# Routed experts: weights in 18 slots instead of two halves, the low halves on VectorE and ScalarE alone, and the code of a single tile ahead of that of a pair

## The chip, the cores and the metric

The kernel runs on one core of one Trainium2 chip. The metric is the time of one execution on the device in microseconds (us); of several executions the median counts. The engines are TensorE (PE for products, PEld for loading their stationary side), VectorE (DVE), ScalarE (ACT), GpSimd (POOL) and SyncE (SP), which issues most transfers. Each runs an instruction stream of its own, in order, and waits on counters (semaphores) that the others raise.

## What is computed

Three stages follow each other: attention with a memory term (4 x 8 heads, 576 rows of 64), a layer of eight experts, and a gated layer.

```python
logits = x @ w_gate                      # x: 2304 tokens x 512
e_idx = np.argmax(logits, axis=1)
for e in range(8):
    mask = e_idx == e
    h = np.maximum(x[mask] @ w1[e], 0.0)         # 512 -> 1024
    ye = h @ w2[e]                               # 1024 -> 512
    out[mask] = gate_w[mask, None] * eom[mask, e, None] * ye
...
gate = 1.0 / (1.0 + np.exp(-(x @ w_gate)))       # 512 -> 1536
return (gate * (x @ w_val) @ w_out)
```

How many tokens an expert has is known only on the device. With these inputs the eight experts have 2, 465, 120, 834, 36, 680, 12 and 155 tokens, that is 1, 4, 1, 7, 1, 6, 1 and 2 tiles of 128.

## The kernel before

All products run on values split in two fp32r halves, a high one (ScalarE copies it, line 1159) and a low one (the rest, a subtraction, line 1166); three products (high x high, high x low, low x high) stand for one. The weights of an expert are eight parts of 128 x 1024: four of w1, four of w2. Each is loaded to one of seven raw buffers, and split to the two halves (`split_hi`, `split_lo`). Two large tiles W[0] and W[1] hold the halves, of even and of odd experts. While expert e runs, the eight parts of expert e + 1 are split (`splits`, `split_part`); of eight low halves POOL takes three (parts 2, 4 and 7) and DVE five. After the last expert's turn come parts of the gated layer's weights (`early_parts`: six parts are converted from 64 bits during expert 7, `convert` on DVE, line 1204 to 1210, low halves on POOL, line 1218).

An expert's tiles run in pairs, and an odd last one alone. `pair` has 152 products, `single` 64 (four layer-1 groups of six, then layer 2, with the turns of h and of the next x between them); with the weight loads that is some 304 and 128 instructions of PE. Both begin with the gather of the next x tiles by POOL (`load_x`, lines 1260 to 1262), turn these tiles near their end (`x_turn`, lines 1270 to 1274) and end with `store_y`: ACT scales the first tile (line 1281), DVE the second (line 1283), and SP stores. In `single` the splits stand at fixed places: SG = (0, 3, 2, 3, 1, 3, 1) steps of `splits` after the loads, after the first relu, in the middle of the second layer-1 group, and so on.

The branches are nested per expert (line 1445): if it has more than one tile, `pair` and then `rest(e, 1)`, which asks at line 1412 whether anything is left, then whether two are; `else` branches with `single` stand behind the whole nest, in reverse order. So in the instruction streams an expert's code is: first pair, second, third and fourth pair, a loop that serves experts of more than eight tiles, and then the single-tile codes. An expert of one tile jumps over all of that, and one with an even number of tiles jumps from its last pair to the nest's end, from there behind the single codes, and on.

The framework counts each engine's finished instructions through all branches. On a path that leaves a block out, each engine waits until its own count is reached (its earlier work is finished) and adds the block's number; SP does the same for the counters of its transfers. This is called a pad here. Code behind a branch waits for the highest count among the paths; if the path taken left that work out, it waits for the pad of the engine that would have done it.

The first single tile's code (expert 0) follows a part of the attention stage in which parts 6 and 7 of expert 0 are split by POOL as one instruction each, part 1 as four (line 672).

Of the kernel before, what the change touches and what calls it, by code (L numbers as in the profile page):

```python
# [18 lines left out]
P = 128  # L19
# [7 lines left out]
NE = 8  # L27
# [99 lines left out]
class Attention:  # L127
# [385 lines left out]
    def run(self, ex, change):  # L513
# [153 lines left out]
        for n in range(8):  # L667
# [4 lines left out]
                lambda e, n=n: ex.split_lo(n, *((self.nc.vector, 1) if e == "DV" else (self.nc.gpsimd, 4 if n < 2 else 1))), needs=[("wh", n)] + late)  # L672
# [401 lines left out]
class Experts:  # L1074
# [67 lines left out]
    def hi_lo(self, part):  # L1142

        kind, a, i = part
        if kind == "e":
            w = self.W[a % 2]
            o = i * 1024 if i < 4 else 8192 + (i - 4) * 1024
            return w[:, o : o + 1024], w[:, o + 4096 : o + 5120]
        n = 3 * i + a
        w, n = (self.Wx, n) if n < 4 else (self.W[0], n - 4) if n < 20 else (self.W[1], n - 20)  # L1150
        o = n * 1024
        return w[:, o : o + 512], w[:, o + 512 : o + 1024]
# [62 lines left out]
    def split(self, n, lo, eng=None):  # L1215
# [26 lines left out]
    def experts(self, ids, cum, start, xn, gather):  # L1242
        tc, nc = self.tc, self.nc
        with ExitStack() as ctx:
# [46 lines left out]


            def layer1(w, n, ms):
                for m in ms:
                    a, o = ((xh, 0), (xh, 4096), (xl, 0))[m // 4]
                    c = o + m % 4 * 1024 + n * 512
                    nc.tensor.matmul(  # L1297
                        pH[n], lhsT=a[:, m % 4, 0:P], rhs=w[:, c : c + 512], start=(m == 0), stop=(m == 11)
# [9 lines left out]
            def layer2(w, n, ms):  # L1308
                for m in ms:
                    a, o = ((hh, 8192), (hh, 12288), (hl, 8192))[m // 4]  # L1310
                    k = m % 4
                    c = o + (n * 4 + k) * 512
                    nc.tensor.matmul(
                        pY[0], lhsT=a[n][:, k * P : (k + 1) * P], rhs=w[:, c : c + 512],
# [3 lines left out]
            def single(e, i, k, splits=iter(())):  # L1318
                w = self.W[e % 2]
# [29 lines left out]
                split(99 * (e == NE - 1))  # L1349


            def inner(w, f):
                p = (*pH, *pT)[f % 4][:, 0 : 2 * P]
                for m in range(12):
                    a, o = ((xh, 0), (xh, 4096), (xl, 0))[m // 4]
                    c = o + m % 4 * 1024 + f * P
                    nc.tensor.matmul(p, lhsT=w[:, c : c + P], rhs=a[:, m % 4, :], start=(m == 0), stop=(m == 11))
# [5 lines left out]
            def outer(w, f):  # L1363
                for t in range(2):
                    q = f % 2 * 256 + t * P
                    for m, (a, o) in enumerate(((hh, 8192), (hh, 12288), (hl, 8192))):
                        nc.tensor.matmul(
                            pY[t], lhsT=a[f % 4 // 2][:, q : q + P], rhs=w[:, o + f * 512 : o + (f + 1) * 512],
# [3 lines left out]
            def pair(e, i, k, splits=iter(()), lead=False):  # L1372
                w = self.W[e % 2]
# [25 lines left out]
            def splits(e):  # L1399
# [4 lines left out]
                for n in range(8):  # L1404
                    self.split_part()
                    yield
                    if n % 2 == 0:
                        yield

            def rest(e, j):  # L1410

                with tc.If(cum[e + 1] > cum[e] + 2 * j):
                    if j > AHEAD:
# [4 lines left out]
                        return  # L1418
# [20 lines left out]
            with tc.manual_schedule():  # L1439
                x_turn(0)  # L1440
                for e in range(NE):
                    if e == NE - 1:
                        first_load()
                    state = dict(self.at), list(self.free), self.loads, self.done
# [304 lines left out]
```

## Time and profile before

| | |
|---|---|
| three runs | 1103.66, 1106.94, 1111.60 us; median 1106.94 us |
| the profiled execution | 1110.49 us, of which the span of the trace is 1108.6 us |
| expert stage in it | about 310 us to 629 us of the span |
| PE busy | 1028.2 us (93%) |
| DVE, ACT, POOL busy | 525.0, 456.2 and 289.1 us |

The trace gives each instruction's start and length, and what ended the idle time of its engine before it. "issue" there is idle time in which the engine waited for nothing that the profile shows. "L1297" is line 1297 of the kernel. The queue named q8 carries PE's instructions in blocks of 16 KB, which is 256 instructions; q14 carries blocks of 8 KB.

### The profile page before, as it was taken

How to read it: one execution, taken by the hardware profiler on the slowest of the kernel's cores; microseconds unless marked ns; L12 is line 12 of the kernel's file. 1: busy time of each engine (PE TensorE's matmuls, PEld its weight loads, DVE VectorE, ACT ScalarE, POOL GpSimd, SP SyncE). 2: the span in 40 equal slices, each digit the busy share in tenths (PEclk: the TensorE clock that was granted, in tenths of full speed). 3: DMA queues.
4: the chain of work that ended last, by engine and by line, in shares of the span. 5: the costliest groups of instructions: out<-in, count | busy, mean ns of one | idle time of the engine just before them, and what ended most of it. 6: DMA issues, size and time to landing. Idle time of an engine off the chain costs nothing. (4 is left out here: it accounts for less than half of the span.)

```text
span 1108.6 us, 17069 instructions
## 1 busy us (share of the span) xinstructions
PE 1028.2 (93%) x6181; PEld 878.6 (79%) x6181; DVE 525.0 (47%) x1263; ACT 456.2 (41%) x1049; POOL 289.1 (26%) x396
## 2 busy tenths in 40 slices
PE   6899899999869699989979789999999999999997
PEld 4567566666559589968968689999899999999996
DVE  5877677676564163246216799931212122121111
ACT  5687686876444253236224455521212221221211
POOL 8677446231374152035115200000100100100101
PEclk9899999999879899999999889999999999999999
DMA  6637445321277164138225455500110100100000
GB/s 123 130 99 172 104 85 131 73 66 36 75 261 257 44 236 136 39 91 295 73 66 149 162 175 196 159 1 1 38 48 1 58 1 1 57 1 1 30 1 28
DMA packets 111899, 102.49 MB, mean 92 GB/s; under 512 B 69520, under 2 KB 86928, under 8 KB 111760
## 3 DMA queue, kind: packets, MB, share of 16 engines
q1 hardware_dynamic: 107888, 88.18, 27.7%
q0 software_dynamic: 3872, 12.62, 3.6%
q8 instruction: 68, 1.11, 0.4%
q14 instruction: 71, 0.58, 0.2%
HBM read 84.49 MB, written 16.28 MB: 91 GB/s over the span
## 5 line engine op out<-in xcount | busy, mean ns | idle before, releaser
L1546 DVE TENSOR_TENSOR G<-G,pT 128x384 f32<-128x384 f32 (+1 forms) x74 | 40.1, 542 | 249.0 <-PE pT L1532 247.5
L1578 POOL DMA_INDIRECT out_dram<-o,rows x18 | 17.5, 971 | 461.7 <-ACT o L1574 212.5
L1553 ACT ACTIVATE Gh<-G 128x384 fp32r<-128x384 f32 (+1 forms) x74 | 38.2, 516 | 162.1 <-DVE G L1546 162.0
L1542 ACT ACTIVATE G<-pH 128x384 f32<-128x384 f32 x72 | 35.4, 491 | 132.4 <-PE pH L1532 132.3
L415 ACT ACTIVATE Sm<-Sm,mx 128x512 f32<-128x512 f32 (+3 forms) x144 | 83.2, 579 | 14.1 <-DVE mx L407 13.6
L407 DVE CUSTOM_DVE_ANT_0 Sm<-Sp,mask 128x512 f32<-128x512 f32 (+3 forms) x144 | 65.2, 481 | 19.6 <-PE T L460 8.1
L1166 POOL TENSOR_TENSOR W<-raw,W 128x1024 fp32r<-128x1024 f32 (+1 forms) x25 | 56.7, 2274 | 66.8 <-ACT W L1159 66.8
L460 PE MATMUL T<-ident,Sm 128*128 128x128 f32 (+1 forms) x400 | 61.2, 287 | 8.9 <-ACT xt L304 3.2
L1563 PE MATMUL pX<-W,Gh 128*128 128x512 f32 x220 | 68.9, 394 | 0.0
L1159 ACT ACTIVATE W<-raw 128x1024 fp32r<-128x1024 f32 x60 | 61.7, 1054 | 13.8 <-DMA y_dram<-y 6.5
L460 PEld LDWEIGHTS T<-ident,Sm 128*128 128x128 f32 (+1 forms) x400 | 44.3, 142 | 21.0 <-ACT xt L304 4.0
L1166 DVE TENSOR_TENSOR W<-raw,W 128x1024 fp32r<-128x1024 f32 x38 | 56.9, 1508 | 6.8 <-ACT W L1159 6.8
L494 PE MATMUL O<-pt,vn 128*64 128x192 f32 (+4 forms) x512 | 59.7, 353 | 0.0
L304 ACT ACTIVATE pt<-T 128x512 f32<-128x512 f32 (+4 forms) x128 | 49.3, 434 | 24.5 <-PE T L460 24.0
L1551 DVE TENSOR_TENSOR Gl<-G,Gh 128x384 fp32r<-128x384 f32 (+1 forms) x74 | 40.4, 546 | 33.9 <-ACT Gh L1553 33.9
L1532 PE MATMUL pT<-xh,W 128*128 128x384 f32 x264 | 52.8, 343 | 2.0 <-DVE G L1546 2.0
L1532 PE MATMUL pT<-yh,W 128*128 128x384 f32 x264 | 51.3, 336 | 0.0
L378 PE MATMUL Sp<-kz,qT 64*128 64x512 f32 (+3 forms) x384 | 49.0, 361 | 1.9 <-DVE kz L351 0.8
L1532 PEld LDWEIGHTS pT<-xh,W 128*128 128x128 f32 x264 | 47.4, 192 | 3.0 <-DVE G L1546 2.2
L1297 PE MATMUL pH<-W,xh 128*128 128x512 f32 x80 | 26.4, 472 | 24.8 <-issue 24.3
L1532 PE MATMUL pH<-yh,W 128*128 128x384 f32 x240 | 47.0, 337 | 1.4 <-DVE xl L1521 1.4
L494 PEld LDWEIGHTS O<-pt,vn 128*64 128x64 f32 (+1 forms) x512 | 30.6, 137 | 21.6 <-issue 13.7
(336 smaller groups left out, 2457.8 us busy)
## 6 DMA issues: line engine op xcount, KB each, us to landing
raw<-in_moe_w_dram SPq DMA_DIRECT2D x60, 512.0 KB, 5.1
raw<-in_moe_w_gate_dram SPq DMA_DIRECT2D x12, 512.0 KB, 5.9
raw<-in_moe_w_val_dram SPq DMA_DIRECT2D x12, 512.0 KB, 3.7
raw<-in_moe_w_out_dram SPq DMA_DIRECT2D x12, 512.0 KB, 4.6
y_dram<-y SPq DMA_DIRECT2D x9, 513.0 KB, 3.5
qn<-in_q_dram SPq DMA_DIRECT2D x32, 128.0 KB, 2.6
kn<-in_k_dram SPq DMA_DIRECT2D x32, 128.0 KB, 2.7
zf<-in_z_prev_dram SPq DMA_DIRECT2D x32, 128.0 KB, 5.3
```

Of the source, the lines that this page charges most:

```text
L304: self.nc.scalar.activation(out, in_, AF.Copy)
L378: nc.tensor.matmul(Sp[:, j, 0:n], lhsT=q[r, a, c * 128 : (c + 1) * 128], rhs=kz[r, k, 0:n], start=(p_ == 0), stop=(p_ == 2), skip_group_ch ...
L407: self.nc.vector.tensor_tensor_reduce(out=self.Sm[pi, n][:, k0:k1], in0=self.Sp[pi, c][:, j if n < 8 else si, 0 : k1 - k0], in1=mask, scal ...
L415: self.nc.scalar.activation(self.Sm[pi, n], self.Sm[pi, n], AF.Exp, scale=-1.0, bias=self.mx[pi, n][:, si : si + 1], accum_out=self.sums[p ...
L460: nc.tensor.transpose(T[:kr, o * 128 : (o + 1) * 128], self.Sm[pi, n][:, i * 128 : i * 128 + kr], self.ident)
L494: nc.tensor.matmul(O[j * 64 : (j + 1) * 64, q0 - q0b : q1 - q0b], lhsT=self.G[gi, "v"][:kr, i, 2 * l + j, :], rhs=PT[:kr, j, i, q0:q1], st ...
L1159: self.nc.scalar.activation(hi, t, AF.Copy)
L1166: eng.tensor_tensor(lo[:, o : o + w], t[:, o : o + w], hi.bitcast(F32)[:, o : o + w], ALU.subtract)
L1532: nc.tensor.matmul(t, lhsT=w[:, k * P : (k + 1) * P], rhs=x[:, k, :], start=(m == k == 0), stop=(m == 2 and k == 3),)
L1546: nc.vector.tensor_tensor(t, t, p, ALU.mult)
L1551: nc.vector.tensor_tensor(l, t, hi.bitcast(F32), ALU.subtract)
L1563: nc.tensor.matmul(po[g][jj], lhsT=a[:, ts], rhs=w, start=(f == 0 and m == 0), stop=(f == NF - 1 and m == 2), skip_group_check=True,)
```

## The change

Four things change. First, the two weight tiles and the small tile Wx become 18 slots of one part each, used in turn; the splits run up to ten parts ahead instead of eight: expert 1 splits ten parts, experts 2 to 5 eight each, expert 6 the last six, so that the first two parts of the next but one expert are always done. Second, all low halves in this stage go to DVE, the early parts of the gated layer too; POOL keeps only parts 1, 6 and 7 of expert 0, and takes each of them in four instructions. Third, `rest(e, 0)` replaces the nest: for each j first "exactly one tile left: `single`", then "two or more left: `pair`, and `rest(e, j + 1)`", two branches in a row without an `else`. Fourth, at the start of `single` and of `pair` each engine gets an instruction that announces where a coming branch will jump (`jump`): from `single` over the pair's code, from `pair` over the next pair's code if no two tiles will be left.

```diff
-                lambda e, n=n: ex.split_lo(n, *((self.nc.vector, 1) if e == "DV" else (self.nc.gpsimd, 4 if n < 2 else 1))), needs=[("wh", n)] + late)
+                lambda e, n=n: ex.split_lo(n, *((self.nc.vector, 1) if e == "DV" else (self.nc.gpsimd, 4))), needs=[("wh", n)] + late)
...
-            w = self.W[a % 2]
-            o = i * 1024 if i < 4 else 8192 + (i - 4) * 1024
-            return w[:, o : o + 1024], w[:, o + 4096 : o + 5120]
+            return self.slot(8 * a + i)
+
+        n = 20 + 3 * i + a
+        o = n % 2 * 512
+        return [t[:, o : o + 512] for t in self.slot(n // 2)]
+
+    def slot(self, n):
+
+        n %= 18
+        w, n = (self.W[n // 8], n % 8) if n < 16 else (self.Wx, n - 16)
+        return w[:, n * 2048 : n * 2048 + 1024], w[:, n * 2048 + 1024 : (n + 1) * 2048]
...
-        self.split_lo(n, self.nc.gpsimd if n % 8 in (2, 4, 7) else self.nc.vector)
+        self.split_lo(n, self.nc.vector)
...
-            (eng or self.nc.gpsimd).tensor_tensor(low, self.float32(n), hi.bitcast(F32), ALU.subtract)
+            self.nc.vector.tensor_tensor(low, self.float32(n), hi.bitcast(F32), ALU.subtract)
...
-                split(99 * (e == NE - 1))
+                split(99)
...
-                for n in range(8):
+                first, last = 8 * e + 8 + 2 * (e > 1), min(8 * e + 16 + 2 * (e > 0), 8 * NE)
+                for n in range(first, last):
                     self.split_part()
                     yield
-                    if n % 2 == 0:
+                    if n % 2 == 0 and last - n > 4:
                         yield
...
-            def rest(e, j):
-                with tc.If(cum[e + 1] > cum[e] + 2 * j):
-                    if j > AHEAD:
+            def jump(label, unless=None):
+
+                tc.mark_branch_hint_location(label, *(() if unless is None else (unless,)), engines=mybir.ALL_ENGINES)
+
+            def rest(e, j, splits):
+
+                more = lambda j: cum[e + 1] > cum[e] + 2 * j + 1
+                if j > AHEAD:
...
-                    with tc.If(cum[e + 1] > cum[e] + 2 * j + 1) as two:
-                        pair(e, within(cum[e] + 2 * j, 2), 2 * j)
-                        rest(e, j + 1)
-                    with two.Else():
-                        single(e, within(cum[e] + 2 * j, 1), 2 * j)
+                state = dict(self.at), list(self.free), self.loads, self.done
+                with tc.If(cum[e + 1] == cum[e] + 2 * j + 1):
+                    jump(f"two{e}_{j}")
+                    single(e, within(cum[e] + 2 * j, 1), 2 * j, splits())
+                self.at, self.free, self.loads, self.done = state
+                with tc.If(more(j), label=f"two{e}_{j}"):
+                    jump(f"two{e}_{j + 1}", more(j + 1) if j < AHEAD else cum[e + 1] > cum[e] + 2 * j + 2)
+                    pair(e, within(cum[e] + 2 * j, 2), 2 * j, splits(), lead=e == j == 0)
+                    rest(e, j + 1, lambda: iter(()))
...
-                    with tc.If(cum[e + 1] > cum[e] + 1) as several:
-                        pair(e, within(cum[e], 2), 0, splits(e), lead=e == 0)
-                        rest(e, 1)
-                    with several.Else():
-                        self.at, self.free, self.loads, self.done = state
-                        single(e, cum[e], 0, splits(e))
+                    rest(e, 0, lambda: splits(e))
```

The products read the same values as before, now through `weights(e)`, which looks up the slot of a part.

## Rows read from the trace of the kernel before

**Rows 1.** The page's first line: the span.

```profile
span 1108.6 us, 17069 instructions
```

**Rows 2.** Waits of PE, whole span (waiting line <- releaser: us in total, times, longest).

```profile
PE pH L1297 <- issue: 24.3, 4, 9.2
PE pH L1514 <- PEq L1412: 3.7, 1, 3.7
```

**Rows 3.** Busy time by engine in two stretches, as the view's columns give it, granted clock.

```profile
504.00:574.00 70.00, 70.00 (x456) 63.74 (x455) 22.71 (x38) 22.23 (x42) 19.22 (x25) 1.00 0.39 133
387.00:402.40 15.40, 15.40 (x64) 12.26 (x65) 9.26 (x11) 7.02 (x9) 5.61 (x3) 0.83 0.40 136
```

**Rows 4.** Timeline, expert 1's end to expert 3's start (start, us, what; idle before, releaser).

```profile
377.14 0.69 ACT L1281 ACTIVATE y<-pY,sid 128x512 f32<-128x512 f32 x1 [1.47 <-issue]
377.83 0.75 DVE L1283 TENSOR_SCALAR y<-pY,sid 128x512 f32<-128x512 f32 x1 [1.32 <-issue]
378.07 0.18 POOL L1260 COPY sid<-xn 128x2 int32<-128x2 int32 x1 [19.41 <-ACTq L1412]
382.95 2.95 ACT L1159 ACTIVATE W<-raw 128x1024 fp32r<-128x1024 f32 x3 [5.13 <-DMA y_dram<-y]
386.97 3.75 PE L1297 MATMUL pH<-W,xh 128*128 128x512 f32 x8 [9.24 <-issue]
...
402.40 1.02 PEld L1357 LDWEIGHTS pH<-xh,W 128*128 128x128 f32 x8 [0.32 <-ACT W L1159]
```

**Rows 5.** Instruction queue of PE, 377.7 to 387 us (packets, MB, share).

```profile
q8 instruction: 3, 0.05, 2.5%
```

**Rows 6.** The same queue, 309.8 to 312.9 us.

```profile
q8 instruction: 1, 0.02, 2.1%
```

**Rows 7.** Timeline, expert 0's start and expert 1's start.

```profile
309.94 0.60 ACT L1273 ACTIVATE xh<-pX 128x512 fp32r<-128x512 f32 x1 [8.10 <-PE pX L1270]
...
312.89 3.75 PE L1297 MATMUL pH<-W,xh 128*128 128x512 f32 x8 [3.04 <-issue]
...
317.93 0.69 DVE L1329 TENSOR_SCALAR h<-pH 128x512 f32<-128x512 f32 x1 [6.67 <-PE pH L1297]
...
331.58 0.74 PE L1357 MATMUL pH<-xl,W 128*128 128x256 f32 x4 [2.31 <-DVE W L1166]
```

**Rows 8.** Timeline, expert 3's end, expert 4, expert 5's start.

```profile
486.64 0.69 ACT L1281 ACTIVATE y<-pY,sid 128x512 f32<-128x512 f32 x1 [2.09 <-issue]
...
489.40 2.10 PE L1297 MATMUL pH<-W,xh 128*128 128x512 f32 x8 [2.85 <-issue]
489.61 2.96 ACT L1159 ACTIVATE W<-raw 128x1024 fp32r<-128x1024 f32 x3 [2.28 <-issue]
...
492.53 0.69 DVE L1329 TENSOR_SCALAR h<-pH 128x512 f32<-128x512 f32 x1 [7.14 <-PE pH L1297]
...
497.78 0.68 DVE L1335 TENSOR_SCALAR h<-pH 128x512 f32<-128x512 f32 x1
498.38 2.18 DVE L1166 TENSOR_TENSOR W<-raw,W 128x1024 fp32r<-128x1024 f32 x1
...
504.13 1.01 PEld L1357 LDWEIGHTS pH<-xh,W 128*128 128x128 f32 x8 [0.33 <-ACT W L1159]
```

**Rows 9.** Timeline, expert 5's end, expert 6, expert 7's start.

```profile
583.79 3.44 PE L1297 MATMUL pH<-W,xh 128*128 128x512 f32 x8 [9.13 <-issue]
...
588.88 2.35 DVE L1166 TENSOR_TENSOR W<-raw,W 128x1024 fp32r<-128x1024 f32 x2
...
598.18 1.01 PEld L1357 LDWEIGHTS pH<-xh,W 128*128 128x128 f32 x8 [0.32 <-ACT W L1159]
```

**Rows 10.** Timeline in expert 7: a conversion step on DVE.

```profile
616.38 1.67 DVE L1208 SCALAR_TENSOR_TENSOR cv_a<-raw,cv_a 128x512 int32<-128x512 int32 x1
```

**Rows 11.** Timeline, expert 1: the second pair's first products, the first pair's last result.

```profile
354.15 1.12 PE L1357 MATMUL pH<-xh,W 128*128 128x256 f32 x8
354.41 0.76 DVE L1283 TENSOR_SCALAR y<-pY,sid 128x512 f32<-128x512 f32 x1 [1.33 <-issue]
```

More of the change, by code (lines that the diff above doesn't have):

```diff
@@ L1213, in halves, with split @@
         return self.hi_lo(("m", n % 3, n // 3))
-    def split(self, n, lo, eng=None):
+    def split(self, n, lo):
         hi, low = self.halves(n)
         if lo:
-            (eng or self.nc.gpsimd).tensor_tensor(low, self.float32(n), hi.bitcast(F32), ALU.subtract)
+            self.nc.vector.tensor_tensor(low, self.float32(n), hi.bitcast(F32), ALU.subtract)
         else:
@@ L1290, in store_y, with weights @@
                 )
+            def weights(e):
+                return lambda i, lo: self.slot(8 * e + i)[lo]
             def layer1(w, n, ms):
                 for m in ms:
-                    a, o = ((xh, 0), (xh, 4096), (xl, 0))[m // 4]
-                    c = o + m % 4 * 1024 + n * 512
+                    a, lo = ((xh, 0), (xh, 1), (xl, 0))[m // 4]
                     nc.tensor.matmul(
-                        pH[n], lhsT=a[:, m % 4, 0:P], rhs=w[:, c : c + 512], start=(m == 0), stop=(m == 11)
+                        pH[n], lhsT=a[:, m % 4, 0:P], rhs=w(m % 4, lo)[:, n * 512 : (n + 1) * 512], start=(m == 0), stop=(m == 11)
                     )
@@ L1318, in single @@
             def single(e, i, k, splits=iter(())):
[L1319 removed]
+                w = weights(e)
                 def split(n):
@@ L1354, in inner @@
                 for m in range(12):
-                    a, o = ((xh, 0), (xh, 4096), (xl, 0))[m // 4]
-                    c = o + m % 4 * 1024 + f * P
-                    nc.tensor.matmul(p, lhsT=w[:, c : c + P], rhs=a[:, m % 4, :], start=(m == 0), stop=(m == 11))
+                    a, lo = ((xh, 0), (xh, 1), (xl, 0))[m // 4]
+                    nc.tensor.matmul(p, lhsT=w(m % 4, lo)[:, f * P : (f + 1) * P], rhs=a[:, m % 4, :], start=(m == 0), stop=(m == 11))
                 b = f % 4 // 2
@@ L1365, in outer @@
                     q = f % 2 * 256 + t * P
-                    for m, (a, o) in enumerate(((hh, 8192), (hh, 12288), (hl, 8192))):
+                    for m, (a, lo) in enumerate(((hh, 0), (hh, 1), (hl, 0))):
                         nc.tensor.matmul(
-                            pY[t], lhsT=a[f % 4 // 2][:, q : q + P], rhs=w[:, o + f * 512 : o + (f + 1) * 512],
+                            pY[t], lhsT=a[f % 4 // 2][:, q : q + P], rhs=w(4 + f // 2, lo)[:, f % 2 * 512 : f % 2 * 512 + 512],
                             start=(f == 0 and m == 0), stop=(f == 7 and m == 2), skip_group_check=True,
@@ L1403, in splits @@
                     return
-                for n in range(8):
+                first, last = 8 * e + 8 + 2 * (e > 1), min(8 * e + 16 + 2 * (e > 0), 8 * NE)
+                for n in range(first, last):
                     self.split_part()
                     yield
-                    if n % 2 == 0:
+                    if n % 2 == 0 and last - n > 4:
                         yield
-            def rest(e, j):
-                with tc.If(cum[e + 1] > cum[e] + 2 * j):
-                    if j > AHEAD:
+            def jump(label, unless=None):
[3 more added lines that the diff above has]
+                if j > AHEAD:
+                    with tc.If(cum[e + 1] > cum[e] + 2 * j, label=f"two{e}_{j}"):
                         with tc.For_i(cum[e] + 2 * j, cum[e + 1], 1) as i:
@@ L1609, in gated @@
                 add(("hi", n), r, {"AC": 0.52}, lambda e, n=n: self.split(n, 0), needs=[("c", n, 3)], uses=[("cva", n)])
-                add(("lo", n), r, {"DV": 0.6}, lambda e, n=n: self.split(n, 1, nc.vector), needs=[("hi", n)], uses=[("cva", n)])
+                add(("lo", n), r, {"DV": 0.6}, lambda e, n=n: self.split(n, 1), needs=[("hi", n)], uses=[("cva", n)])
             def ready(*ns):
```

15 lines of the change are left out of this document (5 added, 10 removed).

## Prediction

> **What bounds the kernel now.** PE is busy for 93% of the span of 1108.6 us [rows 1], so what makes it stand still sets the end. I first looked for places where PE stands still. In the list of waits most of PE's idle time in the expert stage has no releaser: 24.3 us in four pieces ahead of `single`, and 3.7 us ahead of the gated stage, put down to PE's own branches [rows 2]. The timeline then places the pieces: 3.04 us ahead of expert 0 [rows 7], 9.24 ahead of expert 2 [rows 4], 2.85 ahead of expert 4 [rows 8], 9.13 ahead of expert 6 [rows 9]. Each is a place where the code jumps far. Inside the pairs PE never stops: 70.00 of 70 us, over three pairs [rows 3].
>
> What fills them is shown by PE's instruction queue. In the 9.24 us ahead of expert 2 it fetched three blocks [rows 5]; ahead of expert 0, where there is one far jump, one block, in a gap of 3.04 us [rows 6, 7]. So a far jump costs PE about 3 us. From the last pair of expert 1 to `single` of expert 2 there are three: over the next pairs, behind the single codes, over expert 2's pairs. The first can overlap the last products only as far as the pad behind it, which waits for them.
>
> Other engines jump too, over less code. ACT had nothing to wait for in 2.28 us ahead of its first split in expert 4 [rows 8]: that is my price of a far jump of the small engines. A short way is cheap: ACT ended expert 1's last result at 377.14 + 0.69 = 377.83, and POOL, which waits for ACT's pad, started at 378.07 [rows 4]. So 0.24 us covers a branch, a short jump and a pad.
>
> **Part one, the far jumps.** Afterwards a one-tile expert falls into its code. I write E for the end of PE's work in an expert. The next expert's first products wait for the highest counts of x's halves and of the buffers that DVE frees, so for the pads of ACT and DVE. After a pair DVE is last: its result ends at 377.83 + 0.75 = 378.58, E + 0.85 (E = 386.97 - 9.24 = 377.73) [rows 4]. Then come two pads, one for the single code passed by (0.24) and one behind the announced jump. The trace has no announced jump. Bounds: 0.24, as a short one, and 2.28, as a far one; I take 0.3, since the target is announced a whole pair earlier (70/3 = 23 us [rows 3]). So the start is at E + 0.85 + 0.24 + 0.3 = E + 1.4. After a single tile ACT's result comes last: 486.64 + 0.69 = 487.33, with E = 489.40 - 2.85 = 486.55 [rows 8]; with the same two steps E + 0.78 + 0.54 = E + 1.3.
>
> **Part two, `single` with all low halves on DVE.** Prices: one subtraction of 1024 without POOL beside it is 2.35/2 = 1.18 us [rows 9]; a step of 512 (h, hl, xl) 0.6, as the start of the next one shows (497.78 to 498.38) [rows 8]. The first relu can start 492.53 - 489.40 = 3.13 us after PE [rows 8]. With eight parts the order on DVE is h, three parts, hl, h, three parts, hl, one part, xl twice, one part: 6 x 0.6 + 8 x 1.18 = 13.1 us, so DVE ends 16.2 us after PE's start. PE alone would be done at 14. With the pads (0.54) the next expert starts at 16.8 us; DVE, not PE, sets it. Now it is 504.13 - 489.40 = 14.73 us with three parts on POOL [rows 8]. Expert 6 has six parts, four of them ahead of the second relu: 3.13 + 3 x 0.6 + 4 x 1.18 = 9.65 us; from that relu's end (498.46) to the end of PE's work in expert 4 (504.13 - 0.33 = 503.80) it is 5.3 us [rows 8], so E = 14.95, and the next starts 1.3 later, at 16.25. DVE's lone work costs some 2 us a tile. A low half beside POOL is dear now (2.18 us for one [rows 8]), which gives part of it back and is in these sums.
>
> **Part three, the pads between pairs.** Now the second pair's first products follow at 354.15, ahead of the result of the first on DVE, 354.41 to 355.17 [rows 11]. Afterwards each pair comes behind a `single` that is passed by; its first products wait for the pad of DVE, at 355.17 + 0.24 = 355.41. That is 1.26 us for each passage, a wait that is new. There are five: one in expert 1, two in each of experts 3 and 5. Bounds: 0, if the count needed were reached without the pad, and 3.0 each, if PE's short jump over the single code missed its block too [rows 6, 7]; behind these pads wait PE's products alone. I take 1.26, because DVE cannot finish earlier.
>
> **The sum**, each from the end of PE's work in one expert to the first products two experts on:
> - Experts 0 and 1. x's high half ends at 310.54, so PE starts at 310.6 instead of 312.89. The first relu came 5.0 us after the start, in a stretch of low clock [rows 7]; so 315.6 + 13.1 + 0.54 = 329.2. Now expert 1 starts at 328.05 and stands 2.31 us for DVE's last part [rows 7], as if at 330.4. Gain 1.2; I take 1.0, for POOL's parts in four pieces each.
> - Experts 1 to 3: now 402.40 - 377.73 = 24.67; then 1.4 + 16.8 = 18.2. Gain 6.5 [rows 4].
> - Experts 3 to 5: now 504.13 - 486.55 = 17.58; then 1.3 + 16.8 = 18.1. Loss 0.5 [rows 8].
> - Experts 5 to 7: E = 583.79 - 9.13 = 574.66, now 598.18 - 574.66 = 23.52; then 1.4 + 16.25 = 17.65. Gain 5.9 [rows 9].
> - Five passages between pairs: 5 x 1.26 = 6.3 lost.
> - To the gated stage: 3.7 now [rows 2], 1.4 then. Gain 2.3.
>
> 1.0 + 6.5 - 0.5 + 5.9 - 6.3 + 2.3 = 8.9 us.
>
> The rest at nothing. Two parts further ahead: the next expert waits for the pads, and so for all splits, whichever parts they are; if it did not, some 1 us a single tile would come back (in the range). In expert 7 the six low halves move to DVE (6 x 0.6 = 3.6 us), and its steps are no longer stretched beside POOL (one took 1.67 us [rows 10]; by five such steps against 0.7 it would be 5 us); but they come right behind ACT's half and wait for it, and the first conversion waits for SP's pad. I take 0, from -2 to +2. The other index arithmetic, the hints' own issue and the four pieces of parts 6 and 7 lie under PE's work.
>
> [...] The later starts are at full clock in the sums. At the gated stage's start I count nothing; up to 2 us could come.
>
> The profiled execution took 1110.49 us, so the sum gives 1101.6. It lies 3.55 above the median of the three runs, 1106.94; from that: 1106.94 - 8.9 = **1098 us**.
>
> [...]
>
> **Rivals.**
> - *Announced jumps still miss* (the other side). Then each of the eight ends of an expert pays about 2.28 us on DVE or ACT instead of 0.3 [rows 8]: 8 x 2.0 = 16 us, 1098 + 16 = 1114, slower than before. It decides from five misses on (8.9 / 2.0). For it: no row shows an announcement working. Against: even then two of the three far jumps ahead of experts 2 and 6 are gone, and the 9 us there with them [rows 4, 9].
> - *Pads between pairs cost nothing*, PE runs on as now [rows 3]: 1098 - 6.3 = 1092; with the clock's 2 us 1090. For it: the products need nothing of the single code. Against: the framework's counts, as POOL's wait for ACT's pad shows [rows 4].
> - *DVE and the loads fall behind.* ACT's first split waited until 382.95, 5.2 us after E, for a store of results [rows 4]; if such waits stand ahead of the first splits of the three later single tiles, each starts its low halves about 1 us later, and expert 7's conversions come some 2 us late: 1098 + 3 + 2 = 1103, up to 1108.
>
> **How the numbers follow.** The forecast (jumps hidden, pads paid), 1094 to 1102: 0.5. Pads free, 1086 to 1094: 0.2. DVE and loads late, 1102 to 1109: 0.17. Announcements useless, 1109 to 1122: 0.13. A change of 1% is 11 us, about what a measurement can tell here. Faster than 1095.9: all but a little of the second case and a third of the forecast's range, 0.36. Slower than 1118: the upper part of the last, 0.06. Between: 0.58. The range 1087 to 1112 leaves out some 0.03 below and 0.10 above.
>
> **What would show it.** Right: PE goes from expert 1 to 2, and 5 to 6, with an idle of 1 to 2 us, put down to DVE's or ACT's queue; five new idles of about 1.3 us at second and third pairs; `single` of experts 2 and 4 lasting 16 to 17 us, with DVE idle little; no low half over 1.3 us. Wrong: PE's idle there at 3 us or more with a fetch in it (first rival); pairs that follow without idle (second); a first split that waits for a store (third). What would make all wrong is a move of the gated stage's time, which this sum holds fixed.

## The result and the profile after

The changed kernel takes 1117.65 us (median of eight runs, 1113.47 to 1120.64) where the kernel before takes 1107.15 on the same chip: a ratio of 1.0105, with a 95% interval of 1.0078 to 1.0132. The prediction was 1098 us with a range up to 1112: wrong in sign, by some 20 us. The loss is small, about 1%, but clear of the scatter of the runs. The profiled execution of the changed kernel took 1117.78 us, its span is 1116.0.

First again the waits of PE (waiting line <- releaser: us in total, times, longest).

```profile
PE pH L1362 <- ACTq L1431: 15.4, 3, 6.3
...
PE pH L1362 <- DVEq L1431: 8.1, 6, 2.8
...
PE pH L1303 <- SPq L1431: 3.9, 2, 2.0
...
PE pY L1372 <- ACT hh L1365: 2.0, 1, 2.0
...
PE pH L1523 <- DVEq L1435: 1.7, 1, 1.7
```

The 24.3 us without a releaser and the 3.7 us put down to PE's own branches [rows 2] are gone. In their place PE waits for the sequencers of ACT, DVE and SP, which come to their pads late. The largest entry is new: three waits, 15.4 us, ahead of a pair's first products (line 1362), for ACT. The timeline of PE's first products places the waits (start, us, what; idle before, releaser): the second pair of expert 1, then experts 2, 4, 5 and 7.

```profile
357.45 0.83 PE L1362 MATMUL pH<-xh,W 128*128 128x256 f32 x5 [1.06 <-DVEq L1431]
...
383.07 0.70 PE L1303 MATMUL pH<-Wx,xh 128*128 128x512 f32 x2 [1.97 <-SPq L1431]
...
491.62 0.70 PE L1303 MATMUL pH<-W,xh 128*128 128x512 f32 x2 [1.37 <-POOL ic L1265]
...
512.04 1.22 PE L1362 MATMUL pH<-xh,W 128*128 128x256 f32 x4 [6.31 <-ACTq L1431]
...
607.16 1.25 PE L1362 MATMUL pH<-xh,W 128*128 128x256 f32 x7 [3.44 <-ACTq L1431]
```

Ahead of the single tiles PE stands 1.4 to 2.0 us, as forecast, where it stood 9.24, 2.85 and 9.13 [rows 4, 8, 9]. But behind them it stands 3.4 to 6.3 us, where it had run straight on (0.32 and 0.33 [rows 4, 8, 9]). The timeline behind the single tile of expert 2 shows who is late:

```profile
397.29 0.69 ACT L1285 ACTIVATE y<-pY,sid 128x512 f32<-128x512 f32 x1 [1.20 <-issue]
397.68 1.22 DVE L1170 TENSOR_TENSOR W<-raw,W 128x1024 fp32r<-128x1024 f32 x1
402.80 2.08 PE L1362 MATMUL pH<-xh,W 128*128 128x256 f32 x8 [5.60 <-ACTq L1431]
402.88 0.19 POOL L1264 COPY sid<-xn 128x2 int32<-128x2 int32 x1 [16.51 <-ACTq L1431]
```

ACT was done at 397.98 and DVE at 398.90. PE and POOL both wait for ACT until 402.80. ACT's own instruction records, with what its sequencer does between the busy rows (start, length, line, kind), say where it was:

```
397.30 0.06 L1431 COMPARE_BRANCH     the end of the single tile's code
397.84 0.07 L1435 COMPARE_BRANCH     the announced jump
402.42 0.02 L1435 EVENT_SEMAPHORE    the first instruction at its target
```

Between the announced jump's end and the first instruction at its target lie 4.52 us (402.42 - 397.90). That instruction asks for ACT's own count, which was reached at 397.99, so it isn't this count that ACT stood for. Behind experts 4 and 6 it is 5.25 and 2.18 us.

A second loss is in PE's clock. Busy time by engine, granted clock, share of the DMA engines and GB/s, at the start of the pairs of experts 3, 5 and 7:

```profile
402.80:407.00 4.20, 4.20 (x21) 4.20 (x22) 0.42 (x1) 0.38 (x1) 2.56 (x6) 0.56 0.45 138
512.04:516.00 3.96, 3.96 (x19) 3.96 (x20) 0.42 (x1) 0.39 (x1) 2.56 (x6) 0.54 0.39 114
607.20:612.00 4.80, 4.80 (x28) 4.80 (x29) 0.79 (x2) 1.45 (x3) 2.58 (x7) 0.64 0.42 71
```

and of the kernel before, expert 5's first pair:

```profile
504.10:509.00 4.90, 4.90 (x39) 4.79 (x39) 2.66 (x5) 3.56 (x6) 4.23 (x4) 1.00 1.00 344
```

PE is busy all the time in each, but at a granted 0.54 to 0.64 (0.50 from 402.80 to 405.00 us), and does 19 products in 3.96 us, where it did 39 in 4.90 at 1.00.

### The profile page after: what moved, and what is told of

It is laid out like the page before. It is cut to its first block, busy times and chain, and to the rows that moved or that the text cites. A ratio compares the mean times of both kernels' runs of the same rounds, so it can differ in the third digit from the quotient of the medians.

```text
span 1116.0 us, 17561 instructions
## 1 busy us (share of the span) xinstructions
PE 1028.7 (92%) x6181; PEld 875.4 (78%) x6181; DVE 533.9 (48%) x1290; ACT 455.4 (41%) x1049; POOL 220.4 (20%) x375
## 5 line engine op out<-in xcount | busy, mean ns | idle before, releaser
L1362 PE MATMUL pH<-xh,W 128*128 128x256 f32 x288 | 45.5, 306 | 23.4 <-ACTq L1431 15.4
L1170 DVE TENSOR_TENSOR W<-raw,W 128x1024 fp32r<-128x1024 f32 x53 | 63.2, 1220 | 7.6 <-ACT W L1163 7.1
L1362 PEld LDWEIGHTS pH<-xh,W 128*128 128x128 f32 x288 | 42.6, 212 | 28.8 <-ACTq L1431 23.9
L1163 ACT ACTIVATE W<-raw 128x1024 fp32r<-128x1024 f32 x54 | 55.1, 1053 | 12.0 <-DMA raw<-in_moe_w_dram 3.8
L1264 POOL COPY sid<-xn 128x2 int32<-128x2 int32 x28 | 5.4, 194 | 232.9 <-ACTq L1431 162.7
L1541 PEld LDWEIGHTS pT<-yh,W 128*128 128x128 f32 x264 | 46.4, 188 | 3.4 <-DVE G L1555 2.6
L1366 DVE SCALAR_TENSOR_TENSOR hl<-pH,hh 128x256 fp32r<-128x256 f32 x36 | 15.2, 423 | 70.8 <-ACT hh L1365 68.4
```

Of the source, the lines that this page charges most:

```text
L1163: self.nc.scalar.activation(hi, t, AF.Copy)
L1170: eng.tensor_tensor(lo[:, o : o + w], t[:, o : o + w], hi.bitcast(F32)[:, o : o + w], ALU.subtract)
L1362: nc.tensor.matmul(p, lhsT=w(m % 4, lo)[:, f * P : (f + 1) * P], rhs=a[:, m % 4, :], start=(m == 0), stop=(m == 11))
L1541: nc.tensor.matmul(t, lhsT=w[:, k * P : (k + 1) * P], rhs=x[:, k, :], start=(m == k == 0), stop=(m == 2 and k == 3),)
```

## Experiments

The theory from these rows: behind a single tile the announced jump is as dear on ACT as a jump that is not announced, and everything waits for ACT's pad. Its rival: the splits on DVE alone, or ten parts ahead, cost the time. Ratios are to the kernel before on the same chip, with 95% intervals.

**Without announcements.**

```diff
             def jump(label, unless=None):
-                tc.mark_branch_hint_location(label, *(() if unless is None else (unless,)), engines=mybir.ALL_ENGINES)
+                return
```

> The changed kernel without any announcement; all else stays. In the changed kernel ACT's instruction stream stood 4.52, 5.25 and 2.18 us at the announced jump behind the single tiles of experts 2, 4 and 6, and PE 5.60, 6.31 and 3.44 us ahead of the next pairs. Theory A (an announcement given at a single tile's start is of no use by its end): the same three gaps within 1 us, 1114 to 1121 us. Theory B (the announcements work, and what is left is something else, as more code crossed and engines that fetch at once): without them the ends of the pair-ended experts get 2 to 3 us longer too, and PE's far jumps come back, 1122 to 1140 us.

1129.94 us, 1.0278 [1.0223, 1.0334]. The two theories are right at different places. PE's gaps behind experts 0, 1, 5 and 7 grew from 2.77, 1.97, 1.97 and 1.70 to 6.34, 5.46, 4.86 and 4.79 us; those behind the single tiles of experts 2, 4 and 6 are 5.30, 6.03 and 3.31, for 5.60, 6.31 and 3.44. Two of them in the timeline, ahead of expert 2 and behind it:

```profile
381.78 1.19 PE L1303 MATMUL pH<-Wx,xh 128*128 128x512 f32 x2 [5.46 <-DMA y_dram<-y]
...
402.96 1.26 PE L1362 MATMUL pH<-xh,W 128*128 128x256 f32 x4 [5.30 <-ACTq L1431]
```

So announcements are worth having in this kernel, but not for ACT: its jump behind expert 2 took 4.53 us without one, 4.52 with one. Behind expert 4, ACT's jump took 0.45 us here, and PE stood 6.03 us all the same, now put down to its own sequencer; without an announcement it jumps far itself:

```profile
PE pH L1362 <- PEq L1431: 6.0, 1, 6.0
```

PE's own records say so too: its branch behind expert 2's single tile took 0.35 us with an announcement and 5.60 without, and 6.27 without behind expert 4. So PE's announcement works behind the single tiles as well; ACT's wait hides it there.

**Announcements for PE alone.**

```diff
-                tc.mark_branch_hint_location(label, ..., engines=mybir.ALL_ENGINES)
+                tc.mark_branch_hint_location(label, ..., engines=[mybir.EngineType.PE])
```

> The changed kernel with the announcements for PE alone. Without any announcement PE's gaps grew at the ends of experts 0, 1, 5 and 7 (2.77 to 6.34, 1.97 to 5.47, 1.97 to 4.86, 1.70 to 4.79 us), while ACT's jumps behind the single tiles were the same 4.5 us (expert 2), quicker (expert 4, 0.45 for 5.25) or the same 2.6 us (expert 6). Theory A (announcements help PE and do nothing for ACT, DVE, POOL and SP): these four gaps stay at 2 to 3 us, the gap behind expert 4 falls from 6.3 to 2 or 3 us, and the time falls by 3 to 5 us against the changed kernel, a ratio to before of 1.006 to 1.008. Theory B (the small engines need theirs): the gaps behind experts 1, 5 and 7 return to 3 us or more, ratio 1.015 or more.

1116.5 us, 1.0105 [1.0057, 1.0154]. The gaps behind experts 0, 1, 5 and 7 are 2.43, 2.04, 1.98 and 2.20 us: what the announcements gave, they gave on PE. The waits:

```profile
PE pH L1362 <- ACTq L1431: 14.0, 3, 5.4
...
PE pH L1303 <- SPq L1431: 4.0, 2, 2.0
```

The hoped-for 3 to 5 us did not come. Behind expert 4 ACT's announced jump was quick, but its next one, the short way over expert 5's single-tile code, took 4.38 us; why is open. The gap is 5.44 us.

**The announcement late in the single tile.**

```diff
-                    jump(f"two{e}_{j}")
-                    single(e, within(cum[e] + 2 * j, 1), 2 * j, splits())
+                    single(e, within(cum[e] + 2 * j, 1), 2 * j, splits(), lambda: jump(f"two{e}_{j}"))
...
                 split(SG[5])
+                announce()
                 layer2(w, 1, range(12))
```

> The changed kernel, with the announcement of a single tile given some 4 us ahead of the jump, before the last twelve products, instead of at its start, 14 us ahead. Theory A in the form that later fetches push the announced block out: the jumps of ACT fall to 0.4 us, PE's gaps ahead of the pairs of experts 3, 5 and 7 from 5.60, 6.31 and 3.44 to some 2 us each, 1117.7 - 9 = 1108 us. If the announcement is not used at all, or what follows the target is what is missing: no change, 1114 to 1121 us.

1120.79 us, 1.0166 [1.0119, 1.0213]. The gaps are 5.93, 5.75 and 3.19 us, ACT's jumps 4.85, 4.68 and 2.12. Giving it later does not help. The single tiles of experts 2 and 6 took 15.7 and 16.8 us of PE instead of 14.1 and 15.2; why is open.

**The pad ahead of the single tile.** The single tile's code ends with a taken branch over its pad; here it falls through.

```diff
-                with tc.If(cum[e + 1] == cum[e] + 2 * j + 1):
+                with tc.If(cum[e + 1] == cum[e] + 2 * j + 1, preferred_fallthrough_block=False):
```

> The changed kernel with the pad ahead of the single tile's code instead of behind it, so that the single tile falls into the announced jump without a taken branch between the announcement and it. In the changed kernel that branch takes ACT 0.41 us with an announcement open and 0.11 without. If this branch is what spoils ACT's announcement: ACT's jumps behind experts 2, 4 and 6 fall to 0.4 us, PE's gaps from 5.6, 6.3 and 3.4 to some 2 us each, ratio to before 1.001. If not: gaps of 3 to 6 us as before, ratio 1.008 to 1.013.

1127.57 us, 1.0181 [1.0147, 1.0215]. ACT's jumps took 2.95, 5.29 and 2.62 us: the branch in between is not what spoils them. Ahead of experts 2 and 6 the gaps returned to 5.14 and 5.88 us; passing by a single tile now ends with a branch of its own in front of the announced one. Which engine that delays is open.

**An eighth of the weights' bytes.** From expert 3 on this kernel leaves out 112 of each part's 128 partitions.

```diff
+        if kind == "e" and a > 2:
+            dst, src = dst[0:16], src[0:16]
         load = self.nc.sync.dma_start(out=dst, in_=src)
```

> The changed kernel with an eighth of the bytes of the experts' weights loaded from expert 3 on (16 of 128 partitions; the rest keeps old values). Where ACT stood 4.5 and 5.3 us at the jump, the transfers held 93 and 96% of the DMA engines; where it stood 2.2, 36%. If the instruction blocks are slowed by the weights' transfers: ACT's jumps behind experts 2 and 4 fall to 2 to 2.5 us and PE's gaps from 5.6 and 6.3 to 3 to 3.5 us, 5 to 6 us less, and some more where loads were late; ratio to before 1.003 to 1.007. If not: gaps as before, 1.009 or more.

1115.22 us, 1.0062 [1.0025, 1.0099]. ACT's jumps took 2.26, 2.23 and 2.42 us, PE's gaps 3.33, 3.30 and 3.48. The transfers in ACT's three jumps in the changed kernel (the last two columns are the DMA engines' busy share and GB/s):

```profile
397.90:402.40 4.50, 0.00 (x0) 0.00 (x0) 1.00 (x1) 0.08 (x1) 0.00 (x0) 0.70 0.93 310
506.40:511.70 5.30, 0.00 (x0) 0.00 (x0) 1.02 (x1) 0.10 (x1) 0.00 (x0) 0.73 0.96 327
604.40:606.60 2.20, 0.00 (x0) 0.00 (x0) 0.00 (x0) 0.10 (x1) 0.00 (x0) 1.00 0.36 134
```

and in the three gaps of this kernel:

```profile
401.97:405.30 3.33, 0.00 (x1) 0.00 (x1) 1.69 (x2) 0.69 (x1) 0.00 (x0) 0.88 0.16 47
509.39:512.70 3.31, 0.01 (x2) 0.01 (x1) 1.70 (x2) 0.69 (x1) 0.00 (x0) 1.00 0.21 55
605.25:608.70 3.45, 0.00 (x1) 0.00 (x0) 0.00 (x0) 0.69 (x1) 0.00 (x0) 1.00 0.36 130
```

With the DMA engines 93 to 96% busy a jump of ACT took 4.5 to 5.3 us; with 16 to 36%, 2.2 to 2.4. Beside the whole transfers of the weights the jumps behind experts 2 and 4 cost twice as much as beside an eighth of them, 5.3 us more in the two gaps. The times don't tell the two kernels apart (the intervals overlap); the gaps do. Between these shares of the DMA engines the price is not a smooth one: ACT's jumps took 2.95 us at 63% in the run before this one, and 3.39 and 2.41 at 90 and 73% in the kernel with the branches alone (below). My 2.28 us [rows 8] was read with the DMA engines 35% busy (487.33 to 489.61 us), mostly with a store of results, and no load of weights.

**A shorter way.** Codes for two pairs per expert instead of four, so that ACT's way over them is 116 to 118 instructions and not some 198. By my estimate a block of q14 holds 128: in the kernel before, 17 blocks of q8 of 16 KB came from 666.0 to 1075.5 us, in which PE did 2172 products and 2171 weight loads, some 255 instructions a block, and q14's blocks are half as large. Then the same with announcements for PE alone. Experts 3 and 5 run longer here, in the loop, so only the jumps are read.

```diff
-AHEAD = 3
+AHEAD = 1
```

> The changed kernel with codes for two pairs per expert instead of four; tiles beyond the fourth run in the loop, one by one, so experts 3 and 5 take another path and the time of the whole is not compared. What is read are the jumps behind the single tiles of experts 2, 4 and 6: over 116 to 118 instructions of ACT instead of some 198. If the length of the way is what ACT waits for: its jumps fall from 4.52, 5.25 and 2.18 to 0.5 us, PE's gaps ahead of the pairs of experts 3, 5 and 7 from 5.60, 6.31 and 3.44 to 1.5 to 2.5 us. If it is the place (branch, pad, own count): the same 2 to 5 us.

> The same with announcements for PE alone. If an announcement takes the block away that ACT fetched in sequence, ACT's jumps are quick here (0.5 us) and slow, 2 us or more, with announcements for all. If announcements do nothing to ACT: the same in both.

ACT's announced jumps behind experts 2, 4 and 6 (us, and what its records show):

```
changed kernel                        4.52   5.25   2.18
two pairs, announced for all          0.39   4.69   0.38
two pairs, announced for PE alone     0.45   0.45   0.44   behind expert 4 the next, short jump took 4.33
```

Five of six jumps took 0.38 to 0.45 us, so it is the length of the way that ACT had waited for there, not the place. The sixth is not explained by the length: behind expert 4 ACT stood in both kernels, 4.69 us at the jump or 4.33 right behind it, with the weights' transfers running (95 and 100% of the DMA engines); PE stood 5.79 and 5.39 us there. Behind expert 6 PE's gap fell to 1.64 and 1.53 us; behind expert 2, where it now waits for DVE, to 4.76 and 2.24. These two kernels ran once each, which is enough for gaps of this size and not for a time.

Over the short way, less than an estimated block, ACT's jumps took 0.38 to 0.45 us here; over some 198 instructions, in the runs above, 2.1 to 5.3. The exceptions are behind expert 4: 4.69 us over the short way, and 0.44 and 0.45 over some 198 instructions, with announcements for PE alone and with none. What makes the short way cheap is not shown.

**The branches alone, and the weights alone.** First the kernel before with the new branches and announcements, then the changed kernel with the branches of before (nothing else is edited).

```diff
-                    with tc.If(cum[e + 1] > cum[e] + 1) as several:
-                        pair(e, within(cum[e], 2), 0, splits(e), lead=e == 0)
-                        rest(e, 1)
-                    with several.Else():
-                        self.at, self.free, self.loads, self.done = state
-                        single(e, cum[e], 0, splits(e))
+                    rest(e, 0, lambda: splits(e))
```

> The kernel before with the new branches and announcements alone: weights in two halves, splits eight parts ahead, three low halves of eight on POOL as before. If the branches' arrangement carries the loss: 1114 to 1121 us, with PE's gaps of 3 to 6 us ahead of the pairs of experts 3, 5 and 7. If the splits on DVE alone or their ten parts ahead carry it: 1098 to 1108 us.

> The changed kernel with the branches of the kernel before (pairs first, single tiles behind the nest, no announcement): slots, ten parts ahead and DVE alone stay. If the branches carry the loss: like the kernel before, 1103 to 1109 us; DVE's lone splits make the singles 0 to 2 us longer, and the far jumps hide part of it. If the splits carry it: 1114 us or more.

The branches alone: 1119.5 us, 1.0157 [1.0111, 1.0203], with gaps of 4.51, 3.52 and 3.58 us ahead of the pairs of experts 3, 5 and 7 and the five pads of 1.05 to 1.44. The weights alone: 1109.31 us, 1.0058 [1.0032, 1.0083]. The branches carry the loss; the weights part is not free either. The two don't add up to the whole change, 1.0105; why is open. In expert 4 of the second one PE starts at 486.21, and the next pair's products stand at 502.9 to 503.70 for DVE's last low half:

```profile
486.21 0.70 PE L1303 MATMUL pH<-W,xh 128*128 128x512 f32 x2 [2.56 <-issue]
...
503.70 0.75 PE L1362 MATMUL pH<-xl,W 128*128 128x256 f32 x4 [0.80 <-DVE W L1170]
```

That is the DVE-bound single tile of the prediction's second part. In the changed kernel it is covered by ACT's longer wait.

**Filling the gap.** Fourteen products of which nothing is read, at the end of the three single tiles.

```diff
                 split(99)
+                if e in (2, 4, 6) and isinstance(k, int) and k == 0:
+                    for m in range(14):
+                        nc.tensor.matmul(
+                            pH[0], lhsT=hh[0][:, 0:P], rhs=w(4 + m % 2, 0)[:, 0:512], start=(m == 0), stop=(m == 13)
+                        )
```

> The changed kernel with fourteen idle products more at the end of the single tiles of experts 2, 4 and 6 (their result is not read), some 3 us of work where PE would stand and wait for ACT's jump. Behind those gaps (5.60, 6.31 and 3.44 us) the granted clock was 0.56, 0.54 and 0.64 for the first 4 to 5 us of the pairs, and the pairs took about 2 us longer than before the change. If the clock falls because PE stood still that long, the gaps shrink to 2.5, 3.2 and 0.4 us, the pairs start at a granted clock near 1, at the same time or up to 0.5 us later, and the time falls by 4 to 6 us: ratio to before 1.005 to 1.007. If the low clock comes from elsewhere: the same pairs, ratio 1.010.

1120.98 us, 1.0132 [1.0083, 1.018]: no gain. The products took 3.4 us, and the gaps became 2.36, 2.82 and 1.31 us. The clock behind them, in steps of 2 us or a little more, for experts 3 and 7:

```profile
402.66:405.00 2.34, 2.14 (x11) 1.97 (x12) 0.00 (x0) 0.00 (x0) 1.60 (x5) 0.72 0.37 137
405.00:407.00 2.00, 2.00 (x11) 2.00 (x11) 0.42 (x1) 0.70 (x2) 1.16 (x2) 0.50 0.57 152
...
609.70:612.00 2.30, 2.30 (x19) 2.30 (x20) 0.14 (x1) 0.55 (x2) 1.91 (x4) 1.00 0.26 44
```

Behind 1.31 us of standing it stayed at 1.00, and that pair took 26.4 us instead of 28.1. But it started 21.4 us behind the start of its single tile, for 18.6 (the tile took 16.7 us instead of 15.2, and its end was 1.3 us further from the pair), and ahead of the gated stage PE stood 3.61 us, for 1.70; why is open. Behind 2.36 it still fell to 0.50. The form of the theory in which 3 us of filling is enough is refuted; that the low clock follows the gaps stands (0.50 behind 2.36 and 2.82 us, 1.00 behind 1.31).

**The kernel before, with announcements.** Since the announcements pay on PE, they can be had without the new order: its branches stay, and with them there are no pads between the pairs.

```diff
+            def jump(label, unless):
+                tc.mark_branch_hint_location(label, unless, engines=[mybir.EngineType.PE])
+
+            def next_one(e):
+                if e < NE - 1:
+                    jump(f"several{e + 1}", cum[e + 2] > cum[e + 1] + 1)
...
-                with tc.If(cum[e + 1] > cum[e] + 2 * j):
+                with tc.If(cum[e + 1] > cum[e] + 2 * j, label=f"rest{e}_{j}"):
...
+                        jump(f"rest{e}_{j + 1}", cum[e + 1] > cum[e] + 2 * j + 2)
                         pair(e, within(cum[e] + 2 * j, 2), 2 * j)
                         rest(e, j + 1)
                     with two.Else():
+                        next_one(e)
                         single(e, within(cum[e] + 2 * j, 1), 2 * j)
...
+                next_one(-1)
                 x_turn(0)
...
-                    with tc.If(cum[e + 1] > cum[e] + 1) as several:
+                    with tc.If(cum[e + 1] > cum[e] + 1, label=f"several{e}") as several:
+                        jump(f"rest{e}_1", cum[e + 1] > cum[e] + 2)
                         pair(e, within(cum[e], 2), 0, splits(e), lead=e == 0)
```

> The kernel before, with its own branches and weights, and announcements for PE alone: ahead of expert 0 and in each single tile the jump to the next expert's single tile, in each pair the jump that leaves the pairs. If an announcement saves PE the 3 us of one far jump: the gap ahead of expert 0 falls from 3.0 to below 1, those ahead of experts 2 and 6 from 9.2 to about 6, ahead of expert 4 from 2.85 to below 1 and ahead of the gated stage from 3.7 to below 2, together 13 us, ratio to before 0.986 to 0.992. If three jumps in a row lose the announcement, only the single ones gain: 5 us, 0.995.

1097.23 us, 0.9907 [0.9873, 0.9942]: faster than both kernels. Its waits at the single tiles and the first of them in the timeline:

```profile
PE pH L1297 <- issue: 16.2, 4, 6.4
...
377.10 1.19 PE L1297 MATMUL pH<-W,xh 128*128 128x512 f32 x2 [6.19 <-issue]
```

for 24.3 us [rows 2] and 9.24 [rows 4]. The gaps ahead of experts 2 and 6 fell by 3.05 and 2.77 us, that ahead of expert 4 from 2.85 to 0.41, and that of the gated stage from 3.7 to 1.01. Ahead of expert 0 nothing was gained (3.21 for 3.04), though by PE's records the announcement came at 302.31, 2.74 us ahead of the branch at 305.05, which took 3.65; why is open.

**The same for all engines, with one more announcement, and with the new weights part.**

```diff
-                tc.mark_branch_hint_location(label, unless, engines=[mybir.EngineType.PE])
+                tc.mark_branch_hint_location(label, unless, engines=mybir.ALL_ENGINES)
```

> The kernel before with announcements, now for all engines instead of PE alone. The announcements for PE alone gave a ratio of 0.9907. If announcements are of no use to ACT, DVE, POOL and SP, as at the single tiles of the changed kernel: 0.989 to 0.993. If they save these engines their far jumps (ACT 1.88 + 2.92 us behind expert 1): PE waits for no small engine at the far jumps here, so at most 2 us, 0.988. If announced blocks replace the ones that are fetched in sequence: slower, 0.993 or more.

```diff
                         rest(e, 1)
+                        next_one(e)
                     with several.Else():
```

> The kernel before with announcements for PE alone, and one more where the code leaves the pairs, between the first and the second of the three far jumps ahead of experts 2 and 6: the third jump's target. The gaps there were 9.24 and 9.13 us without and 6.19 and 6.36 with the first jump announced. If the third fetch can run beside the second: some 3 us each, gaps of 3 to 4 us, ratio to before 0.985 to 0.988. If a fetch only starts when the one before it is done, or the announcement comes too late: 0.989 to 0.993.

> The slots, the ten parts ahead and the low halves on DVE alone, with the branches of before and the announcements for PE alone (all but the one ahead of expert 0, which saved nothing). Without announcements this weights part cost 1.0058 on the branches of before: its single tiles took 17.5 us from start to the next pair instead of 14.7 to 15.4. If that cost stays when the far jumps are shorter: 0.996 to 1.000. If the far jumps hid more of it: 1.000 to 1.004.

For all engines: 1098.79 us, 0.994 [0.9915, 0.9965]. One more: 1095.42, 0.9899 [0.9861, 0.9937], with gaps of 6.21 and 5.81 us ahead of experts 2 and 6 (6.19 and 6.36 without it), so announcing the third far jump at the second did not save the 3 us expected. With the new weights part: 1100.54, 0.9937 [0.9911, 0.9964]. The intervals of the four overlap; none shows that more than the announcements for PE is worth adding to the kernel before. With the weights part 0.996 to 1.000 was expected; it came out below, and its cost beside the announcements for PE alone isn't clear of the runs' scatter.

## Why the prediction was wrong

The prediction's sum, stretch by stretch, each between the same two points of the two profiled executions (us, gain positive). The end points are PE's starts and ends of the rows above and of [rows 4, 7, 8, 9]; the expert stage begins with the first turn of x (308.76, then 306.26) and ends with the gated stage's first turn (628.94, then 636.92). In the kernel before, expert 1's first pair is counted from 330.4, as in the prediction: its first eight products ran at 328.05, and the next ones stood 2.31 us [rows 7].

| stretch | before | after | forecast | measured |
|---|---|---|---|---|
| start to expert 1's first pair | 21.6 | 20.8 | +1.0 | +0.9 |
| expert 1's pairs | 47.3 | 54.1 | -1.3 | -6.8 |
| end of expert 1 to expert 3's first pair | 24.7 | 21.7 | +6.5 | +3.0 |
| expert 3 | 84.2 | 87.4 | -2.5 | -3.3 |
| end of expert 3 to expert 5's first pair | 17.6 | 21.8 | -0.5 | -4.2 |
| expert 5 | 70.5 | 74.5 | -2.5 | -4.0 |
| end of expert 5 to expert 7's pair | 23.5 | 20.6 | +5.9 | +2.9 |
| expert 7 to the gated stage | 30.8 | 29.8 | +2.3 | +1.0 |
| sum | | | +8.9 | -10.5 |

That the measured sum equals the difference of the medians, 10.5 us, is chance. The two profiled executions differ by less, 7.3 us (1110.49 and 1117.78): in that of the changed kernel the stages ahead took 2.5 us less and those behind 0.6.

- *Part one, the step that failed: 0.3 us for an announced jump.* Ahead of the single tiles it held: PE started 1.97, 1.37 and 1.97 us behind the end, for 1.4 and 1.3; the 0.6 more is SP's pad. There the far way is PE's, and PE's announcement works. Behind the single tiles it is ACT's, and ACT's announcement saves nothing. The choice between my bounds of 0.24 and 2.28 was made with the argument that the target is announced long ahead, with no row for it. Nor was the upper bound high enough: the jumps took 2.18 to 5.25 us, and the far way that 2.28 was read from had no weights' transfers beside it. What came instead, behind each of the three single tiles, is ACT's far jump at its full price. By the forecast the pairs behind would have started 16.8, 16.8 and 16.25 us behind the single tiles' starts, so at 399.87, 508.42 and 604.78; they started at 402.80, 512.04 and 607.16. That is 2.9 + 3.6 + 2.4 = 8.9 us, as much as the whole gain of the sum.
- *I looked for the far ways ahead of the single tiles and gave the way behind them one number.* In the kernel before, a first single tile is followed by the next nest at once, and no engine jumps far between them: PE's pause was 0.32 or 0.33 us [rows 4, 8, 9]. The new order moves the way over the pairs from ahead of the tile to behind it, for all engines. The sum counted what PE no longer does, and not that quicker splits let the weights' transfers run just there: 255 GB/s through expert 2's single tile (383.0 to 397.2 us), for 136 then [rows 3].
- *Part two held.* DVE's last low half ended 15.8 us behind PE's start in experts 2 (398.90) and 4 (507.42), for 16.2; the low halves took 1.22 us.
- *Part three held:* five idles of 1.05 to 1.07 us at the second and third pairs, for 1.26. The second rival, free pads, is out.
- *"The later starts are at full clock in the sums" failed.* At 0.54 to 0.64 for 4.0 to 4.8 us each, the three pairs lost, by my estimate, 1.85 + 1.8 + 1.7 = 5.4 us (length times what is missing to 1). Expert 1's first pair had 0.81 over 9 us and 0.79 over 8, 3.4 us more. The old order put its long gaps ahead of single tiles, the new one ahead of pairs. No run shows the up to 2 us that the prediction left open at the gated stage's start and that its second rival's 1090 takes: the clock there was 0.50 before (628.90 to 631.00 us) and 1.00 after (636.90 to 639.00), and the stages behind took 0.6 us less. The busy times of expert 1's first pair, with the clock third from the end:

```profile
327.00:336.00 9.00, 8.84 (x54) 8.41 (x54) 0.42 (x1) 0.38 (x1) 2.24 (x4) 0.81 0.75 277
337.00:345.00 8.00, 6.76 (x32) 5.46 (x33) 6.73 (x9) 5.54 (x9) 0.00 (x0) 0.79 0.55 178
```

- *The third rival, in part,* at another place than it named. In expert 1, ACT's first split waits for SP, and PE's products behind it for 2.0 us. The timeline of ACT, with the wait in brackets:

```profile
336.49 1.06 ACT L1163 ACTIVATE Wx<-raw 128x1024 fp32r<-128x1024 f32 x1 [5.72 <-SPq L1431]
337.45 0.36 ACT L1365 ACTIVATE hh<-pH 128x256 fp32r<-128x256 f32 x1
```

  SP was not held up by its jump, but by its own transfers, whose counters its pad waits for. SP's records, with the last landing of the transfers that each counter stands for:

```
327.65 0.07 L1435 COMPARE_BRANCH     SP's announced jump
332.00 0.02 L1435 EVENT_SEMAPHORE    a transfer's counter, last landing 331.98
334.79 0.02 L1435 EVENT_SEMAPHORE    the next counter, last landing 334.77
335.37 0.02 L1435 EVENT_SEMAPHORE    the third, last landing 335.36
```

  This is a second term that the sum put at nothing: a pad of SP, with loads under way, ahead of ACT's splits.
- *The first rival* named the cause (announced jumps still miss, 16 us, 1114) and had 0.13. It had the place wrong: it took all eight ends of an expert at 2.0 us, where PE's are saved and three of ACT's cost up to 5.25. PE waited for three such jumps, all of ACT; by the rival's rule (from five on) they would not have turned the sign, and it was their price and the clock that did.

The terms together: 8.9 (starts behind the single tiles) + 5.4 + 3.4 (clock) + 2.0 (expert 1's stall) + 1.2 (SP's pads) = 20.9 us lost beyond the forecast, less 1.0 at the pads between pairs: 19.9, where 19.4 were lost (8.9 + 10.5). The 0.5 too much isn't placed; the clock's terms are the roughest. The two experiments on the price bear on the first term (two of its three gaps fell with fewer bytes, two of three with a shorter way); that the clock would stay up without the gaps was shown for one pair alone.

## What to carry to other kernels

Count a far jump for every engine that others wait for, not only for the one that sets the end, and price it with the transfers that will run beside it: here 2.1 to 2.7 us where ACT stood with the DMA engines up to 36% busy, and 3.4 to 5.3 with them 89% busy or more (between these, 2.95 at 63% and 2.41 at 73%; two jumps behind expert 4 took 0.44 and 0.45). An announcement was worth about 3 us (2.4 to 3.6) at the far jumps of PE read here, but for the one ahead of expert 0 in the kernel before, and nothing that showed at ACT's (4.52 us with one behind expert 2, 4.53 without); what it is worth to DVE, POOL and SP was not read. So it pays to add it where the code is, before the code is moved to suit it. A gap ahead of a busy stretch cost twice here: 3.4 to 6.3 us of standing, and 0.54 to 0.64 of the clock for 4.0 to 4.8 us behind it. And a pad that waits for transfers under way holds up what waits for the pad: ACT for 5.72 us here.

## What the runs showed of the hardware

- Instruction fetches ran beside the data: from 397.9 to 402.5 us three blocks of q14, the small engines' queue, and one of PE's took 2.2 and 1.3% of the DMA engines' time, 604 packets of data 89.0%. ACT's jumps behind experts 2 and 4 took 4.52 and 5.25 us with 310 to 327 GB/s running, 2.26 and 2.23 with 47 to 55.
- An announcement helped PE and not ACT in these runs. Ahead of expert 2 PE's gap was 1.97 with it and 5.46 without, and behind expert 2 PE's own branch took 0.35 with it and 5.60 without; ACT's jump behind expert 2 was 4.52 with it, 4.53 without, 4.38 with announcements for PE alone, and 4.85 with a late one. Why is open.
- The same jump of ACT, behind expert 4, took 0.45 us without announcements, 0.44 with announcements for PE alone and 5.25 with them for all engines. Why is open.
- A clock of 0.50 followed gaps of 2.4 to 6.3 us ahead of pairs, and none followed 1.31 us ahead of a pair or 1.97 ahead of expert 2's single tile (1.00 from 383 to 385 us). In the kernel before, a gap of 2.85 ahead of expert 4's single tile had the first eight products in 2.10 us [rows 8], at 1.00 (489.40 to 494.00), and one of 9.24 ahead of expert 2's had them in 3.75 [rows 4], at 0.50 (387 to 391); so the length of the gap alone doesn't say it.
